# Order and tile shape of two small matmul groups ahead of a denominator, and the semaphore that a last multiply carries

## Chip, cores and metric

The kernel runs on one core of one Trainium2 chip. The metric is the device time of one execution in microseconds (us); a run also leaves a profile of one execution, whose span is about 1.6 us shorter than the device time (139.54 against 141.17 in the profiled run of the kernel before). Most executions agree within a few tenths of a microsecond (the kernel before: 141.01 to 141.78).

## The reference

```python
xn = layernorm(x)                                   # x: 2048 tokens x 448
q, k, v = split_heads(xn @ wqkv)                    # 16 heads of 28
phi = lambda t: where(t > 0, t + 1, exp(t)) + 1e-6
kv  = einsum("bhsd,bhse->bhde", phi(k), v)
z   = einsum("bhsd->bhd", phi(k))                   # sum of the keys over tokens
num = einsum("bhqd,bhde->bhqe", phi(q), kv)
den = einsum("bhqd,bhd->bhq", phi(q), z) + 1e-6
s   = merge_heads(num / den) @ wo
g   = silu(relu(xn @ w1 + b1)**2 @ w2 + b2)         # hidden size 1792
out = x + s * g
```

## The kernel before

The kernel records operations, and a small scheduler sets each engine's order and hands out the program's eight PSUM banks (`pb` in the traces): a bank keeps a sum of TensorE (PE) until another engine has read it, and only then goes to the next sum. PE takes its operations in the order in which they are added. Below are the parts that the change touches.

The hidden layer (h) and the second product (w_2, `gg`) run as phases: two sums side by side, one on rows 0 to 63 of the array, one on rows 64 to 127. Their tile shape is 64x128 (rows x columns).

```python
def token_sum(c):                   # xn^T phi(k), c = 3 is the last 64 rows
    for si in range(NT):            # NT = 16 token tiles
        if c < 3:
            ...                     # 128x128 tiles
        else:
            r = slice(64 * (si % 2), 64 * (si % 2) + 64)
            last = e.matmul(
                ps(b)[r, 0:D], xn[:, si, 384:448], pk_of(si), start=(si < 2), stop=(si >= NT - 2)
            )

def z_heads():                      # z per head, from zb, the keys summed over token tiles
    b = Buf("Z")
    def f(e, _):
        for r in range(4):
            for h in (0, 1):
                c, n = r * P + 64 * h, 1 + r // 3
                last = e.matmul(
                    ps(b)[half[h], r : r + n], zb[:, c : c + 64], ones[:, 0:n], start=(r == 0), stop=True,
                    skip_group_check=True,
                )
        return last
    add("pe", f, ["zb", "ones"], [b], 0.5)
    ...                             # VectorE: zsb = z * zmask
    add("dve", zops, [b, "zmask"], ["zsb"], 0.28)

def den():                          # denominators: 8 + 12 matmuls on 128x32 tiles, weights zsb
    ...

def finish(si, b, c):               # out tile = s (PSUM) * g
    ...
    if c.stop == D and c.start:     # the last multiply of the kernel
        op.lastly = "pe"            # this engine's wait stands last, on the instruction itself

# the order on PE
for i in range(3):
    phase((tail_h[i], K4), (tail_h[i + 3], K4))
g0, g1 = gg(0), gg(1)
for i in range(3):
    if i == 2:
        phase((g0, C), (g1, C))
    phase((tail_h[i + 3], K3), (tail_h[i], K3))
phase((g1, C), (g0, C))
z_heads()
token_sum(3)
den()
...
token_sum(0)                        # 128x128
```

An operation of this program with several waits gets separate wait instructions for all but one (EVENT_SEMAPHORE in the trace; 28 of them on VectorE in the profile before); the remaining wait is carried by the instruction itself. `lastly` picks that one.

## Time and profile before

| | before |
|---|---|
| median of 3 runs | 141.18 us (141.01 to 141.78) |
| profiled span | 139.54 us |
| first matmul of the 64x128 stream | 8.50 us |
| from there to the first 128x128 token sum | 69.05 us |
| from there to the last matmul's start | 59.36 us |
| from there to the end | 2.64 us |

The last four rows are my cut of the trace, by the starts of single matmuls; they add up to the span up to rounding. I call them head, middle, rest and tail. In a timeline a line gives start, length, engine, source line, operation, output and inputs, tile rows x columns, sizes and count. I call the time between the starts of like matmuls, pairs or waves in an unbroken row their stream: 0.216 us for 512 columns and 0.189 for 448 in the trace before. A matmul's recorded length is longer (about 0.38 and 0.35 us), so holes are found from starts: previous start plus stream against the next start. Tiles that run side by side form a pair (two, with starts 0.002 to 0.020 us apart in the trace before) or a wave (four, within 0.011). A number with three decimals is a start or an end in the trace's records, which a timeline prints with two.

### The profile page before, as it was taken

The page shows a single profiled execution, that of the slowest core. Times are in us where ns is not written, and L with a number is a line of the kernel's source. Part 1 is how long each engine was busy: PE and PEld are TensorE (multiplying, and loading weights), DVE is VectorE, ACT ScalarE, POOL GpSimd, SP SyncE. Part 2 cuts the span into 40 slices and gives each one's busy share as a digit, 9 for nine tenths or more (in the row PEclk, how much of TensorE's full clock was granted, in tenths as well). Part 3 has the DMA queues.
Part 4 walks back from the last instruction along what each step waited for, and adds up shares of the span by engine and source line. Part 5 has one row for each costly group of instructions (what it writes and reads, how often), then busy time and mean ns, then how long its engine had stood idle before and what let it go on. Part 6 is the DMA issues. An engine that isn't in the chain of part 4 may idle for free.

```text
span 139.5 us, 3096 instructions
## 1 busy us (share of the span) xinstructions
PE 136.6 (98%) x1255; PEld 72.4 (52%) x1255; DVE 92.3 (66%) x225; ACT 78.3 (56%) x153; POOL 26.8 (19%) x35
## 2 busy tenths in 40 slices
PE   9999999999999999999999999999999999999993
PEld 2484455555555555555555455645555555555472
DVE  3989797898888996889995900219836072452743
ACT  4779789788988878979788912512033030300221
POOL 2810000000000000000893000000001429092670
DMA  6997957999823300000000148970000102112132
GB/s 199 244 334 216 88 158 183 359 273 138 141 43 70 61 9 5 0 19 5 0 0 0 37 116 180 165 113 2 0 0 5 66 0 97 39 62 69 36 100 66
DMA packets 20353, 12.90 MB, mean 92 GB/s; under 512 B 9524, under 2 KB 19956, under 8 KB 20340
## 3 DMA queue, kind: packets, MB, share of 16 engines
q1 hardware_dynamic: 18332, 11.52, 35.8%
q10 hardware_dynamic: 2008, 1.19, 4.6%
q8 instruction: 10, 0.16, 0.5%
q14 instruction: 3, 0.02, 0.1%
HBM read 8.78 MB, written 2.10 MB: 78 GB/s over the span
## 4 chain that ended last, share of the span: by engine, by line
PE 95%; DVE 2%; DMA 2%; ACT 0%; issue 0%; DVEq 0%
PE pb L960 31%; PE pb L693 30%; PE pb L646 9%; PE pb L1028 8%; PE pb L727 7%; PE pb L677 6%; DMA x_tok<-in_A_x_dram 2%; PE pb L733 1%; PE pb L532 1%; DVE st L466 1%; PE pb L820 1%; PE pb L781 1%; PE pb L858 0%; DVE mv L467 0%; DVE xn L996 0%; PE pb L851 0%
## 5 line engine op out<-in xcount | busy, mean ns | idle before, releaser
L693 PE MATMUL pb<-xT,w 64*128 64x512 bf16 (+2 forms) x408 | 51.9, 365 | 0.0
L960 PE MATMUL pb<-w,r 64*128 64x448 bf16 (+3 forms) x406 | 44.9, 343 | 0.0
L702 ACT ACTIVATE r<-pb,b1f 128x512 bf16<-128x512 f32 x56 | 35.1, 688 | 3.7 <-PE pb L693 3.7
L693 PEld LDWEIGHTS pb<-xT,w 64*128 64x128 bf16 (+1 forms) x408 | 25.2, 94 | 19.3 <-issue 0.3
L960 PEld LDWEIGHTS pb<-w,r 64*128 64x128 bf16 (+1 forms) x406 | 23.1, 95 | 19.6 <-issue 0.7
L936 ACT ACTIVATE gbuf<-gbuf 128x448 bf16<-128x448 bf16 (+1 forms) x16 | 8.8, 567 | 36.3 <-DVE gbuf L971 35.7
L971 DVE TENSOR_TENSOR gbuf<-pb,b2b 128x448 bf16<-128x448 f32 (+1 forms) x16 | 9.3, 610 | 29.7 <-PE pb L960 29.7
L1007 POOL TENSOR_TENSOR xn<-xn,x_tok 128x448 bf16<-128x448 bf16 x15 | 15.1, 1032 | 46.3 <-DVE xn L996 46.3
L646 PE MATMUL pb<-w_qkv,xT 64*128 64x512 bf16 (+1 forms) x106 | 18.1, 377 | 0.0
L677 PE MATMUL pb<-xT,w_qkv 64*128 64x512 bf16 x84 | 15.6, 376 | 0.0
L710 DVE TENSOR_TENSOR r<-r 128x512 bf16<-128x512 bf16 x42 | 14.3, 419 | 0.0
L393 POOL MEMSET kvm<- 128x2048 bf16 x1 | 1.8, 1805 | 59.2 <-DVE zb L671 59.2
L1028 PE MATMUL pb<-msb,pqT 64*128 64x448 bf16 (+3 forms) x93 | 10.9, 343 | 0.0
L466 DVE BATCH_NORM_STATS2 st<-x_tok 128x6 f32<-128x448 bf16 x16 | 9.3, 612 | 2.4 <-DMA x_tok<-in_A_x_dram 2.3
L634 DVE SCALAR_TENSOR_TENSOR qk<-pb,qk 128x512 bf16<-128x512 f32 x16 | 10.6, 685 | 0.2
L624 ACT ACTIVATE qk<-pb 128x512 bf16<-128x512 f32 x16 | 8.9, 595 | 3.1 <-PE pb L646 2.5
L996 DVE TENSOR_TENSOR xn<-pb,gbuf 128x448 bf16<-128x448 f32 (+2 forms) x17 | 9.2, 591 | 1.8 <-ACT gbuf L936 1.3
L646 PEld LDWEIGHTS pb<-w_qkv,xT 64*128 64x128 bf16 (+1 forms) x106 | 7.1, 94 | 5.7 <-ACT xT L546 0.5
L727 PE MATMUL pb<-qk,xn 128*128 128x448 bf16 x48 | 9.3, 353 | 0.0
L677 PEld LDWEIGHTS pb<-xT,w_qkv 64*128 64x128 bf16 x84 | 6.3, 94 | 4.4
L711 ACT ACTIVATE r<-r 128x512 bf16<-128x512 bf16 x14 | 8.3, 635 | 0.0
L624 ACT ACTIVATE pqT<-pb 128x512 bf16<-128x512 f32 x12 | 6.8, 597 | 2.7 <-PE pb L693 1.6
(72 smaller groups left out, 101.9 us busy)
## 6 DMA issues: line engine op xcount, KB each, us to landing
out_dram<-xn SPq DMA_DIRECT2D x15, 112.0 KB, 1.7
w<-in_B_w_dram SPq DMA_DIRECT2D x1, 1568.0 KB, 10.3
x_tok<-in_A_x_dram SPq DMA_DIRECT2D x3, 448.0 KB, 3.8
xT<-rows ACTq DMA_DIRECT2D x6, 112.0 KB
w<-in_B_w_dram SPq DMA_DIRECT2D x1, 576.0 KB, 5.5
xT<-rows SPq DMA_DIRECT2D x5, 112.0 KB
w_o<-in_A_wo_dram SPq DMA_DIRECT2D x1, 392.0 KB, 11.4
w_qkv<-in_A_wqkv_dram SPq DMA_DIRECT2D x1, 384.0 KB, 3.5
```

Source lines behind the costliest of these rows:

```text
L466: add("dve", lambda e, _: e.bn_stats(st6[:, si, :], x_tok[:, si, :]), [("x", si)], [("st", si)], 0.58),
L624: add("act", lambda e, _: e.activation(out=slot, in_=src(), func=AF.Exp), [buf, "actw"], [tile], 0.6)
L634: lambda e, _: e.scalar_tensor_tensor(out=slot, in0=src(), scalar=1.0 + 1e-6, in1=slot, op0=ALU.add, op1=ALU.max),
L646: return e.matmul(ps(b)[:, 0:512], xT[half[h], c, si * P : (si + 1) * P], w_qkv[half[h], c, 384 : 2 * D], start=start, stop=stop,)
L677: return e.matmul(ps(b)[:, 0:512], w_qkv[half[h], c, m * P : (m + 1) * P], xT[half[h], c, g * 512 : (g + 1) * 512], start=start, stop=stop,)
L693: return e.matmul(ps(b)[:, c0 : c0 + n], w_1[half[h], c, fi * P : (fi + 1) * P], xT[half[h], c, t : t + n], start=start, stop=stop,)
L702: lambda e, _: e.activation(out=slot, in_=ps(b)[:, 0:512], func=AF.Relu, bias=b1f[:, fi : fi + 1]),
L710: return e.tensor_tensor(out=slot, in0=slot, in1=slot, op=ALU.mult)
L727: last = e.matmul(ps(b)[:, 0:D], xn[:, si, c * P : (c + 1) * P], pk_of(si), start=(si == 0), stop=(si == NT - 1),)
L960: return e.matmul(ps(b)[:, 0:n], r2[half[h], fi, si * P : (si + 1) * P], w_2[half[h], fi, c], start=start, stop=stop)
L1007: eng, lambda e, _: e.tensor_tensor(out=ob, in0=ob, in1=x_tok[:, si, c], op=ALU.add),
L1028: return e.matmul(ps(b)[:, 0:n], q, m, start=start, stop=stop)
```

## The change

The intent is to save changes of tile shape on PE: z takes the 64x128 shape of the phases and moves among them; the token sum of the last 64 rows takes the 128x32 shape of the denominators that follow it; and the last multiply no longer has a separate wait for ScalarE.

```diff
+        zlow = sb("zlow", [P, 5], f32)
@@ token_sum
-                        r = slice(64 * (si % 2), 64 * (si % 2) + 64)
-                        last = e.matmul(
-                            ps(b)[r, 0:D], xn[:, si, 384:448], pk_of(si), start=(si < 2), stop=(si >= NT - 2)
-                        )
+                        for i in (0, 1):
+                            r = 64 * (si % 2) + 32 * i
+                            last = e.matmul(
+                                ps(b)[r : r + 32, 0:D], xn[:, si, 384 + 32 * i : 416 + 32 * i], pk_of(si),
+                                start=(si < 2), stop=(si >= NT - 2), skip_group_check=True,
+                            )
@@ z_heads
-            b = Buf("Z")
+            bs = Buf("Z"), Buf("Z")
-                        c, n = r * P + 64 * h, 1 + r // 3
+                        n = 1 + r // 3
-                            ps(b)[half[h], r : r + n], zb[:, c : c + 64], ones[:, 0:n], start=(r == 0), stop=True,
+                            ps(bs[h])[:, r : r + n], zb[half[h], r * P : (r + 1) * P], ones[half[h], 0:n],
... VectorE: zlow = bs[0]; zlow = bs[1] + zlow; zsb = zlow * zmask
@@ finish
-                op.lastly = "pe"
+                op.lastly = "act"
@@ order on PE (behind the first three tail_h phases)
+        z_heads()
         g0, g1 = gg(0), gg(1)
@@ behind the last w_2 phase
         phase((g1, C), (g0, C))
-        z_heads()
         token_sum(3)
```

More of the change, by code (lines that the diff above doesn't have):

```diff
@@ L755, in f @@
                     for h in (0, 1):
-                        c, n = r * P + 64 * h, 1 + r // 3
+                        n = 1 + r // 3
                         last = e.matmul(
-                            ps(b)[half[h], r : r + n], zb[:, c : c + 64], ones[:, 0:n], start=(r == 0), stop=True,
-                            skip_group_check=True,
-                        )
-                return last
-            add("pe", f, ["zb", "ones"], [b], 0.5)
+                            ps(bs[h])[:, r : r + n], zb[half[h], r * P : (r + 1) * P], ones[half[h], 0:n],
+                            start=(r == 0), stop=True, skip_group_check=True,
+                        )
+                return last
+            add("pe", f, ["zb", "ones"], list(bs), 0.25)
+            add("dve", lambda e, _: e.tensor_copy(zlow[:, :], ps(bs[0])[:, 0:5]), [bs[0]], ["zlow"], 0.12)
+            add(
+                "dve",
+                lambda e, _: e.tensor_tensor(out=zlow[:, :], in0=ps(bs[1])[:, 0:5], in1=zlow[:, :], op=ALU.add),
+                [bs[1], "zlow"], ["zlow"], 0.12,
+            )
             def zops(e, _):
-                z = ps(b)[:, 0:5]
+                z = zlow[:, :]
                 z = bass.AP(tensor=z.tensor, offset=z.offset, ap=list(z.ap) + [[0, 32]])
                 return e.tensor_tensor(out=zsb[:, :, :], in0=z, in1=zmask[:, :, :], op=ALU.mult)
-            add("dve", zops, [b, "zmask"], ["zsb"], 0.28)
+            add("dve", zops, ["zlow", "zmask"], ["zsb"], 0.28)
         def fold_wv():
```

## The prediction

Passages of the text below are cut. One of them is a term of the sum: z's time in line, the author's estimate. The path after came to 2.69 us, the gain on PE to 0.14 and the whole sum to 0.20; the terms of the path that still stand (0.10 + 1.52 + 0.86 + 0.10) come to 2.58, and the cut term was the other 0.11. The spacing of 256-column waves is 0.109 us in the trace (76.682 to 76.791), not 0.107; that would add 0.004 to the path.

> **What bounds the kernel now.** I read the page first (busy times, slices, the chain that ended last), then the chain of waits in order of time for the two stretches that the diff touches, then the timeline of the TensorE in those stretches, in windows narrow enough to see single starts.
>
> ```profile
> span 139.5 us, 3096 instructions
> PE 136.6 (98%) x1255; PEld 72.4 (52%) x1255; DVE 92.3 (66%) x225; ACT 78.3 (56%) x153; POOL 26.8 (19%) x35
> PE 95%; DVE 2%; DMA 2%; ACT 0%; issue 0%; DVEq 0%
> ```
>
> TensorE (PE) is the bound: 98% busy and 95% of the chain. A stretch saved on another engine is worth nothing before the last matmul; a stretch saved on PE is worth itself, as long as nothing else catches up. The measured time, 141.18 us, is the span and about 1.7 us outside it. "Busy" hides small holes, because each record lasts longer than its stream (a 448-column matmul is recorded as 0.35 us, but 14 pairs of them take 2.65 us, 0.189 us a pair). So I looked for late starts: where a matmul or pair starts later than the previous start plus its stream. From 8.5 us to 136.9 us the trace has only a handful, each at a change of the tile's shape. Three stand in the stretch that the diff rewrites (timeline of PE; columns: start us, length us, engine, line, operation, tile rows*columns):
>
> ```profile
> 74.50 0.37 PE L960 MATMUL pb<-w,r 64*128 64x448 bf16 x2
> 74.80 0.29 PE L757 MATMUL pb<-ones,zb 128*64 128x1 bf16 x8
> 74.95 1.68 PE L733 MATMUL pb<-qk,xn 128*64 128x448 bf16 x16
> ...
> 76.28 0.35 PE L733 MATMUL pb<-qk,xn 128*64 128x448 bf16 x2
> 76.56 0.40 PE L851 MATMUL pb<-pqR,zsb 128*32 128x256 bf16 x8
> 76.79 0.82 PE L858 MATMUL pb<-pqT,zsb 128*32 128x512 bf16 x12
> 77.22 0.39 PE L858 MATMUL pb<-pqT,zsb 128*32 128x512 bf16 x4
> 77.54 0.36 PE L727 MATMUL pb<-qk,xn 128*128 128x448 bf16 x1
> ```
>
> The reader is to see: the last pair of 64x128 tiles starts at 74.50 and 74.52, so its stream is over at about 74.71, and the z sums (128x64) start at 74.80: 0.09 late. The last 128x64 pair starts at 76.28 and is over at 76.47; the 128x32 matmuls start at 76.56: 0.09 late. Their last wave starts at 77.22, takes 0.216 (the spacing of 512-column waves), is over at 77.44; the 128x128 matmul starts at 77.54: 0.10 late. The profile blames the second hole on a wait:
>
> ```profile
> 76.56 0.12 PEld L851 LDWEIGHTS pb<-pqR,zsb 128*32 128x32 bf16 x8 [0.36 <-DVE zsb L768]
> 75.98 0.32 DVE L768 TENSOR_TENSOR zsb<-pb,zmask 128x160 bf16<-128x160 f32 x1
> ```
>
> But zsb was done at 76.30, before the stream was, and the hole has the size of the others. I take it for a change of shape, not a wait. At the end of the kernel the chain of waits has these pieces (start us, us, what):
>
> ```profile
> 136.89 0.31 ACT gbuf L936
> 137.21 0.03 issue
> 137.24 0.02 DVEq L277
> 137.26 0.04 issue
> 137.30 0.34 DVE xn L996
> ```
>
> ScalarE's silu is over at 137.20; the multiply starts 0.10 later, after a separate wait instruction of VectorE (DVEq) and another issue gap. The multiply before it, whose own wait is on ScalarE, starts 0.04 after its silu (silu 135.86 + 0.44 = 136.30, multiply at 136.34).
>
> [...] The trace agrees, at about 0.09 to 0.10 us a change: the three above, and later 93.89 + 0.19 = 94.08 against 94.18. [...] The z sums stream one or two columns, and here their four pairs take 74.80 to 74.95, 0.15 us, 37 ns a pair[...]. [...] The trace shows it run ahead: the five wait instructions of the denominator's matmuls run at 74.9 to 75.3, while those matmuls start at 76.56. [...] The two multiplies above agree: 0.04 against 0.10.
>
> **The change, part by part.**
>
> z sums on halves. Removed: eight 128x64 matmuls at 74.80. Added: eight 64x128 matmuls (same count, one to two columns), between the first three and the next three h phases, near 67.47, into two banks, as two sums over 64 rows each; VectorE then copies one (5 columns), adds the other, and multiplies by the mask. On PE: 64x128 is the shape of the stream around them, so no change of shape comes in. [...] On VectorE: two small operations of about 0.18 us each (a 128x64 copy is 0.18 here), 0.36 us, inside a stretch where VectorE only squares r tiles and later sits idle 1.83 us before 74.91. Off the path.
>
> Last 64 rows of the token sum on 32-column tiles. Sixteen matmuls of 64 columns, two side by side, become 32 of 32 columns, four side by side. Before: 8 pairs at 0.189 = 1.51 us. After: 8 waves of four at 0.189 = 1.51 us, provided that four run together. The denominator's matmuls do that already: waves of four 512-column matmuls every 0.216 us. So the stream itself gains nothing, but it now has the shape of the denominator's matmuls behind it, and the change of shape between them goes: minus 0.09. The first wave after a change also comes about 0.01 late for its second (76.56 to 76.68 is 0.12 where 256 columns take 0.107); with one change fewer this goes too.
>
> The path before, from the end of the last 64x128 stream to the first 128x128 matmul: 74.71 to 77.54 = 2.83. After: [...] change of shape 0.10, token sum 1.52, denominators 2 x 0.107 + 3 x 0.216 = 0.86, change of shape 0.10: 2.69. Gain 0.14 us [...].
>
> Last multiply. Its wait on TensorE becomes the separate instruction, and ScalarE's is on the multiply itself. TensorE's last matmul (start 136.90) is done about 0.06 before the silu, so the separate wait is passed while the silu still runs. The gap of 0.10 becomes about 0.04: gain 0.06 us, wholly on the path since only the last residual add and the last store follow.
>
> Sum: 0.14 + 0.06 = 0.20 us, 0.14% of 141.18. Predicted 140.98 us.
>
> **The rivals.** Rival A, a new wait: the two z banks. The built order shows that the z sums take two banks that ScalarE must first empty, and that the first w_2 phase (68.77 before) takes those same two after VectorE has read them. ScalarE's four relus end at 64.43 + 2.42 = 66.85, zb is ready at 66.71 (and VectorE's new order has one zacc add of 0.66 less in front of it), z is due at 67.47: 0.6 us to spare. z is done by about 67.75; copy and add end by 68.2, or 68.5 if the four squares ahead are not moved earlier; the w_2 phase is due at 68.88: 0.4 to 0.7 to spare. If the first margin fails PE stalls some tenths and the gain is gone, 141.2 to 141.5.
> Rival B: the four 32-column tiles don't run together, since neighbours share the same keys or the loads double. Two at a time would be 16 x 0.189 = 3.0 us, 1.5 us lost, 142.5. The denominators speak against it.
> Rival C: the waits of the denominators are exposed, as twice the instructions now stand in the queue ahead of them. Five waits at about 0.1 are 0.5 us; [...].
> Rival D: the hole at 76.56 was a wait for zsb. Then too it goes, since zsb is ready some 6 us earlier; the number is the same, but the 128x64 to 128x32 change would not be its cause.
>
> **Range and chances.** The parts give 0.10 to 0.25 us of gain. The three runs of before spread from 141.01 to 141.78, more than the whole effect, so the range is run spread: 140.6 to 141.4. Faster by over 2% would need 2.8 us, which is nowhere in the diff; slower by over 2% needs rival B at nearly full serialisation. Chances: 0.005 faster, 0.985 within 2%, 0.01 slower.
>
> **What would show it.** In the changed kernel's timeline of PE: z pairs near 67.5 as 64x128 matmuls [...]; 32 token-sum matmuls over 1.51 us with one hole of 0.1 before them; the denominators' first matmul 0.19 after the last wave's start, without a hole; from the end of the w_2 phase to the first 128x128 token sum about 2.58 us; the last multiply about 0.04 after the silu, and no separate wait in the chain between. Wrong if PE shows a hole at z or at the first w_2 phase (A), waves wider than 0.189 (B), or a hole at the denominators (C); if the profile's span falls by less than 0.1 or by more than 0.3, a term of the sum is mis-sized.

## The result, and the profile after

The changed kernel took 141.07 us (median of 6 runs, 140.91 to 141.23) against 141.36 us for the kernel before (6 runs, 141.01 to 141.78, the three of the table above among them). The ratio is 0.9979 with a 95% interval from 0.9959 to 0.9999. Every ratio here is the mean time of one kernel's fast runs over the mean time of the fast runs of the kernel before, so it is not quite the ratio of the medians. A run is slow when it lies over 1.5% above the fastest of its kernel; none here did, and every profile told of has a granted TensorE clock of 1.0 in its record.

From the page of the changed kernel, busy times (the span is 139.4 us, and PE has 95% of the chain that ended last):

```profile
PE 136.4 (98%) x1271; PEld 69.3 (50%) x1271; DVE 92.9 (67%) x227; ACT 78.2 (56%) x153; POOL 22.9 (16%) x35
```

PE is still the bound, with 16 matmuls more and 0.2 us of busy time less. The next fence is the timeline of PE in narrow windows: first z in its new place, then the stretch that the prediction took apart.

```profile
67.31 0.38 PE L694 MATMUL pb<-xT,w 64*128 64x512 bf16 x2
67.52 0.25 PE L760 MATMUL pb<-ones,zb 64*128 64x1 bf16 x8
67.62 0.37 PE L694 MATMUL pb<-xT,w 64*128 64x512 bf16 x1
...
74.67 0.36 PE L969 MATMUL pb<-w,r 64*128 64x448 bf16 x2
74.96 1.70 PE L735 MATMUL pb<-qk,xn 128*32 128x448 bf16 x32
...
76.29 0.36 PE L735 MATMUL pb<-qk,xn 128*32 128x448 bf16 x4
76.48 0.39 PE L860 MATMUL pb<-pqR,zsb 128*32 128x256 bf16 x8
...
77.13 0.39 PE L867 MATMUL pb<-pqT,zsb 128*32 128x512 bf16 x4
77.45 0.36 PE L728 MATMUL pb<-qk,xn 128*128 128x448 bf16 x1
```

z starts exactly one stream after the pair before it (67.31 + 0.216) and the next h pair starts 0.104 us later: no hole at z, and 26 ns for each of its four pairs. The 32 matmuls of the token sum start at 74.96, which is 0.09 to 0.10 late (74.67 + 0.19 = 74.86), and take 1.52 us to the denominators' start, as eight waves of 0.189 should. The denominators start 0.19 after the last wave: the hole of 0.09 that stood here before is gone. The last hole, ahead of 77.45, is there as before.

The chain of waits at the end (start us, us, what):

```profile
136.80 0.31 ACT gbuf L945
137.12 0.04 issue
137.15 0.34 DVE xn L1005
```

The separate wait of VectorE no longer stands between the silu and the multiply: 0.04 us in place of 0.10. A separate wait is still there, but now it waits for TensorE. It ran from 137.086 to 137.107, and the silu ended at 137.108.

What now holds the multiply is most likely that wait. In all ten profiles, with either order, the multiply starts 44 to 45 ns after the end of its separate wait instruction. The two multiplies ahead of it carry ScalarE's wait themselves, with their other waits long done, and start 31 to 33 ns after the end of their silu in all ten. So about 0.01 us of the gap seems to be left to the wait for TensorE. No run here tests it.

In the cut by starts, before against after: head 8.50 and 8.57, middle 69.05 and 68.89, rest 59.36 and 59.36, tail 2.64 and 2.57. The middle gives 0.16 and the tail 0.06, together 0.22 us. Some 0.02 of the 0.16 is the uneven start of one pair: the two matmuls of the last w_2 pair start 0.020 apart in the profile before, and 0.003 to 0.009 apart in both profiles of the changed kernel and in e3 below. Up to the first 128x128 token sum e3 runs the same PE program as the kernel before, and its middle is 69.03. The head, which nothing in the diff touches, happened to be 0.07 longer in this profile, so the spans differ by only 0.15. In a second profile of the same changed kernel (e5 below) the head was 8.44, the middle 68.88 and the rest 59.36.

### The profile page after: what moved, and what is told of

It reads as the page before. It is cut to its first block, busy times and chain, and to the rows that moved or that the text cites. A ratio compares the mean times of both kernels' runs of the same rounds, so it can differ in the third digit from the quotient of the medians.

```text
span 139.4 us, 3131 instructions
## 1 busy us (share of the span) xinstructions
PE 136.4 (98%) x1271; PEld 69.3 (50%) x1271; DVE 92.9 (67%) x227; ACT 78.2 (56%) x153; POOL 22.9 (16%) x35
## 4 chain that ended last, share of the span: by engine, by line
PE 95%; DMA 2%; DVE 2%; ACT 0%; issue 0%
PE pb L969 31%; PE pb L694 30%; PE pb L647 9%; PE pb L1037 8%; PE pb L728 7%; PE pb L678 6%; DMA x_tok<-in_A_x_dram 2%; PE pb L735 1%; PE pb L533 1%; DVE st L467 1%; PE pb L829 1%; PE pb L790 1%; PE pb L867 0%; DVE mv L468 0%; DVE xn L1005 0%; ACT gbuf L945 0%
## 5 line engine op out<-in xcount | busy, mean ns | idle before, releaser
L694 PEld LDWEIGHTS pb<-xT,w 64*128 64x128 bf16 (+1 forms) x408 | 23.3, 94 | 21.0 <-DVE qk L635 0.3
L666 DVE TENSOR_TENSOR zacc<-zacc,qk 128x448 f32<-128x448 f32 x13 | 8.1, 623 | 0.3
```

Of the source, the lines that this page charges most:

```text
L694: return e.matmul(ps(b)[:, c0 : c0 + n], w_1[half[h], c, fi * P : (fi + 1) * P], xT[half[h], c, t : t + n], start=start, stop=stop,)
```

## The experiments

The theory: PE pays about 0.1 us for each change of tile shape, whatever is ready, and the change takes one away; z costs 26 ns a pair, as in the profile after; the separate wait costs 0.06. The main rival was that the hole ahead of the denominators had been a wait for zsb, as the profile says. Two batches of four kernels ran, each batch on one chip with its own runs of the kernel before (11 of them in each). All gave correct results.

| run | median us | ratio to before | 95% interval | middle us | silu end to multiply us |
|---|---|---|---|---|---|
| e1 z alone | 141.28 | 0.9991 | 0.9970 to 1.0013 | 69.00 | 0.10 |
| e2 token sum's tiles alone | 141.36 | 0.9999 | 0.9977 to 1.0022 | 69.22 | 0.10 |
| e3 last multiply alone | 141.18 | 0.9989 | 0.9968 to 1.0009 | 69.03 | 0.04 |
| e4 alternating shapes | 142.05 | 1.0039 | 1.0019 to 1.0060 | 69.71 | 0.04 |
| e5 changed kernel again | 140.94 | 0.9985 | 0.9971 to 0.9998 | 68.88 | 0.04 |
| e6 z moved, old form | 141.45 | 1.0011 | 0.9994 to 1.0027 | 69.11 | 0.04 |
| e7 z in halves, old place | 141.44 | 1.0017 | 1.0002 to 1.0032 | 69.31 | 0.04 |
| e8 z ten times | 142.03 | 1.0056 | 1.0037 to 1.0076 | 69.82 | 0.04 |

The kernel before had a median of 141.49 us in the batch of e1 to e4 and of 141.26 in that of e5 to e8. Effects below about 0.2% can't be read from the times, only from the traces.

### e1: z moved, the rest as before

```diff
 # the changed kernel, with
-    32-column tiles in token_sum(3)
+    the 64-column tiles of before
-                op.lastly = "act"
+                op.lastly = "pe"
```

> The changed kernel with the token sum back on 64-column tiles and the last multiply as before: z alone is moved. My theory (the hole ahead of the denominators is a change of tile shape): zsb is ready some 8 us early and the hole of 0.09 us ahead of the denominators' first matmul stays all the same; from the first matmul of the last w_2 pair to the first 128x128 matmul 2.88 us (before 3.04, changed kernel 2.78), z in line 0.10, so a gain over before of about 0.05 us, ratio 0.9996. Rival D (the hole was a wait for zsb): the hole is gone, the stretch is 2.78, gain 0.15 us, ratio 0.999.

Timeline of PE, and of its weight loads (PEld), at the denominators:

```profile
76.77 0.36 PE L734 MATMUL pb<-qk,xn 128*64 128x448 bf16 x2
77.05 0.40 PE L858 MATMUL pb<-pqR,zsb 128*32 128x256 bf16 x8
...
77.05 0.12 PEld L858 LDWEIGHTS pb<-pqR,zsb 128*32 128x32 bf16 x8 [0.36 <-issue]
```

zsb was done at 68.68 + 0.41 = 69.09, eight microseconds early, and the hole is still there: 76.77 + 0.19 = 76.96 against 77.05 (95 ns by single starts, 96 before). The same idle time that the profile had put down to zsb is now put down to "issue". The stretch from the last w_2 pair to the first 128x128 matmul is 2.90 us (2.88 expected). The 0.02 more is in the second pair of the token sum, which starts 0.213 behind the first in place of 0.189. So the hole was a change of shape, and the wait for zsb that the profile named was not its cause.

### e2: 32-column tiles alone

```diff
 # the kernel before, with the token_sum part of the diff only
```

> The kernel before with nothing but the 32-column token sum; z stays where it was, on 128x64 tiles. My theory: as many changes of shape as before (64x128, 128x64, 128x32, 128x128), only the middle one moves to stand ahead of the token sum, 0.09; no hole ahead of the denominators as long as zsb (ready at about 76.30) comes before they are due (about 76.56); stretch from the last w_2 pair to the first 128x128 matmul 3.02 to 3.05 us, gain 0.00, ratio 1.000. If the 32-column tiles themselves were faster, the stretch would fall below 2.9; if they don't run four together it would be 4.5.

```profile
74.72 0.37 PE L962 MATMUL pb<-w,r 64*128 64x448 bf16 x2
75.02 0.29 PE L759 MATMUL pb<-ones,zb 128*64 128x1 bf16 x8
75.23 1.70 PE L734 MATMUL pb<-qk,xn 128*32 128x448 bf16 x32
76.76 0.39 PE L853 MATMUL pb<-pqR,zsb 128*32 128x256 bf16 x8
```

The token sum takes 1.53 us to the denominators, without a hole between them, but z and the token sum now have different shapes: from z's first matmul to the token sum's first it is 0.22 us, where it was 0.15 before. The stretch is 3.02 us, against 3.04. One hole has moved; none has gone. By one measure for all, from the end of the last w_2 pair's stream to the first 128x128 matmul, with z's time added where z was moved, it is 2.83 us before (2.83 in e3), 2.81 in e1, 2.81 in e2 and 2.69 in the changed kernel (2.69 in e5). So z moved saves 0.02 alone, the narrow tiles 0.03 alone, and both together 0.14. The counts of changes of shape fit: three on this path before, in e1 and in e2, and two in the changed kernel. (The middle of this run is longer than that of before, because PE waited 0.20 us for ScalarE at 16.7 us, long ahead of the changed part. That wait is in one profile only.)

### e3: the last multiply alone

```diff
 # the kernel before, with
-                op.lastly = "pe"
+                op.lastly = "act"
```

> The kernel before with nothing but ScalarE's semaphore on the last multiply itself. My theory: from the end of the last silu to the multiply's start 0.04 us instead of 0.10, no separate wait in the chain, gain 0.06 us, ratio 0.9996, too small for the timed rounds to show. Rival (the multiply is held by TensorE's last matmul, or by something else): the gap stays 0.10.

```profile
137.27 0.31 ACT gbuf L936
137.58 0.04 issue
137.62 0.34 DVE xn L996
```

The separate wait is gone from the chain and the gap is 0.04 us, as expected. Here too the wait for TensorE ended, at 137.571, only just before the silu, at 137.572. The tail, from the last matmul's start to the end, is 2.58 us against 2.64 with the old order. The timed ratio of 0.9989 does not contradict it, but can't show it either.

### e4: seven changes of shape more

```diff
 # the changed kernel, token_sum(3)
-                        for i in (0, 1):
-                            r = 64 * (si % 2) + 32 * i
+                        n = 64 if (si // 2) % 2 == 0 else 32
+                        for i in range(64 // n):
+                            r = 64 * (si % 2) + n * i
     ... tiles of n columns in place of 32
```

> The changed kernel with the token sum's eight pairs of tiles alternately on 64-column and 32-column tiles: the same sums, seven changes of shape more. My theory (about 0.10 us a change: 0.09 of hole and 0.01 in the second wave): the stretch from the last w_2 pair to the first 128x128 matmul is 2.78 + 0.7 = 3.5 us, the time 0.7 us longer than the changed kernel's, ratio to before about 1.003. Rival (a hole comes from waits, not from shapes): no holes between the pairs, 2.8 us, ratio 0.998.

```profile
75.01 0.38 PE L736 MATMUL pb<-qk,xn 128*64 128x448 bf16 x2
75.32 0.68 PE L736 MATMUL pb<-qk,xn 128*32 128x448 bf16 x6
75.62 0.68 PE L736 MATMUL pb<-qk,xn 128*64 128x448 bf16 x5
```

(Each line starts at one of the alternating groups; its count runs on into the next.) The groups start about 0.31 us apart instead of 0.189. The stretch is 3.60 us against 2.78, so seven changes cost 0.82, or 0.117 us each: more than the 0.10 that I took. The time agrees: 0.39% over before, where the changed kernel is 0.15% to 0.21% under it, some 0.54% to 0.60% or 0.8 us. This is the one run in which the cost of a change of shape is clear of the noise of the times.

### e5: the changed kernel again

The edit is none; it is the yardstick of e6 to e8.

> The changed kernel once more, on the chip of the next three, so that they are compared with it in the same rounds: 0.15 to 0.3 us less than before, ratio 0.998 to 0.999; the stretch from the last w_2 pair to the first 128x128 matmul 2.78 us again, z in line 0.10, silu to multiply 0.04.

The stretch is 2.78 us, z takes 0.103, the gap ahead of the multiply 0.04, and the ratio is 0.9985. The two batches of the changed kernel agree.

### e6: z in the new place, in the old form

```diff
 # the changed kernel, with z_heads() as before (128x64 tiles, one bank), called in the new place
```

> The changed kernel with z in its new place but in the old form (128x64 tiles, one bank, no addition). My theory: two changes of shape come into the 64x128 stream, so z takes 0.09 + 0.15 + 0.10 = 0.34 us of it instead of 0.10; the time 0.24 us longer than the changed kernel's, about that of before. Rival (the form of z does not matter, only its place): 0.10 to 0.15 us, the time of the changed kernel.

```profile
67.78 0.38 PE L694 MATMUL pb<-xT,w 64*128 64x512 bf16 x2
68.08 0.29 PE L760 MATMUL pb<-ones,zb 128*64 128x1 bf16 x8
68.31 0.39 PE L694 MATMUL pb<-xT,w 64*128 64x512 bf16 x2
```

From the end of the stream before z (67.78 + 0.22 = 68.00) to the next h pair it is 0.31 us (0.34 expected), where the halves take 0.10. The middle is 0.22 us longer than in e5 (69.11 against 68.88, from unrounded values), so z on halves is what keeps the shape of the stream. The scheduler also moved one eviction (a copy out of PSUM) from ScalarE to VectorE in this kernel and one squaring of r the other way; PE shows no hole from it. The ratio to e5 is 1.0011 / 0.9985 = 1.0026, or 0.37 us, which is of the right sign and larger than the trace has it; the two intervals overlap. This profile's head was also long, 9.04 us.

### e7: z on halves, in the old place

```diff
-        z_heads()
         g0, g1 = gg(0), gg(1)
...
         phase((g1, C), (g0, C))
+        z_heads()
         token_sum(3)
```

> The changed kernel with z on its two 64-row halves but in the old place, behind the last w_2 phase. My theory: no change of shape more than in the changed kernel, but zsb now comes from three operations of VectorE behind two evictions of gbuf, ready at about 76.85 where the denominators are due at about 76.4: a true wait of 0.4 us ahead of them, no longer the 0.09 of a change; stretch from the last w_2 pair to the first 128x128 matmul 3.3 us, time 0.4 us longer than the changed kernel's and 0.2 longer than before. Rival (place does not matter): stretch 2.89 (z in it), time of the changed kernel.

Timelines of PE and VectorE (DVE):

```profile
75.06 1.70 PE L735 MATMUL pb<-qk,xn 128*32 128x448 bf16 x32
76.92 0.29 PE L860 MATMUL pb<-pqR,zsb 128*32 128x256 bf16 x4 [0.17 <-DVE zsb L777]
...
75.08 1.16 DVE L980 TENSOR_TENSOR gbuf<-pb,b2b 128x448 bf16<-128x448 f32 x2 [1.84 <-PE pb L969]
76.16 0.15 DVE L767 COPY zlow<-pb 128x5 f32<-128x5 f32 x1
76.34 0.16 DVE L770 TENSOR_TENSOR zlow<-pb,zlow 128x5 f32<-128x5 f32 x1
76.54 0.33 DVE L777 TENSOR_TENSOR zsb<-zlow,zmask 128x160 bf16<-128x160 f32 x1
```

This is what a true wait for zsb looks like. The three operations stand behind two evictions, zsb is done at 76.87, and the denominators start at 76.92, although the token sum's stream was over 0.34 us earlier with the same tile shape on both sides. PE itself, not only the weight loads, is shown idle with zsb as the releaser. The stretch is 3.23 us (3.3 expected). So the two parts of the z edit need each other: on halves z costs two operations more on VectorE (0.15 and 0.16 us here), and only the early place hides them.

### e8: z ten times

```diff
-                for r in range(4):
+                for r in 10 * list(range(4)):
```

> The changed kernel with the eight z matmuls issued ten times over (each time from the start flag, so the result is the same). My theory (about 26 ns a pair, on the path): z takes 1.04 us of the stream, the time 0.94 us longer than the changed kernel's, ratio to it 1.0067. Rival (z hides behind the 512-column stream or in the queue): the time of the changed kernel.

```profile
67.37 1.16 PE L760 MATMUL pb<-ones,zb 64*128 64x1 bf16 x80
68.37 0.37 PE L694 MATMUL pb<-xT,w 64*128 64x512 bf16 x1
```

Eighty matmuls, that is 40 pairs, take 1.00 us of the stream: 25 ns a pair. The ratio to e5 is 1.0056 / 0.9985 = 1.0071, or 1.0 us. The middle is 0.94 us longer than in e5 (69.82 against 68.88), for 36 pairs more: z's cost is wholly on the path and is not hidden behind the streams around it.

## Why the prediction was right

Point by point, by its own steps:

- TensorE as the bound: the rest of the trace behind the changed part, from the first 128x128 token sum to the last matmul, is 59.36 us in the kernel before, in the changed one and in all eight experiments. Whatever was saved or lost ahead of it went through unchanged.
- z in line (the cut term, 0.11 of the 2.69): 0.15 us before, 0.104 in the first profile after, 0.103 in the second, and e8 shows 25 ns a pair when it is repeated.
- Token sum's stream unchanged and one change of shape fewer: 1.52 us and no hole at the denominators. From the end of the w_2 phase (74.86) to the first 128x128 matmul it is 2.59 us in both profiles; 2.58 was forecast.
- The gain on PE of 0.14, the cut term in it: 0.14 by the prediction's own path (2.83 to 2.69), in both profiles of each order; 0.16 by the middle, of which 0.02 is the uneven pair. The hole that went was 0.09 to 0.10, as read, but e4 measures 0.117 per added change.
- The last multiply for 0.06: 0.06, and e3 shows it alone. One reading behind it was off, and here there was luck: the wait for TensorE was to be passed 0.06 ahead of the silu's end, but that counted from the modelled end of the last matmul (137.043 in the changed kernel). The wait instruction starts 0.043 after that end and takes 0.021, so the margin was 0.001. A little later, and the gain would have shrunk.
- Sum 0.20 us: 0.20 by the prediction's own path, 0.22 by the cut; 0.3 and 0.2 us by the two timed ratios, with intervals that reach almost to zero. The forecast of 140.98 us against 141.07 measured says little by itself, since the kernel before moved by as much between its batches.
- Rival A (a new wait at the two z banks): it did not occur. z was issued without a hole, and the addition that frees the second bank was done at 68.18, where the w_2 phase started at 68.92.
- Rival B (32-column tiles not four together): refuted by the eight waves of 0.189.
- Rival C (the denominators' waits exposed): refuted. The five wait instructions ran at 75.2 to 75.6, 0.8 us ahead of the matmuls that they guard.
- Rival D (the hole was a wait): refuted by e1. The profile puts the two other holes before down to waits as well, of weight loads for ScalarE (`r` ahead of 74.80, `at` ahead of 77.54), but what it names was done at 74.56 and 77.22, ahead of the ends of the streams at 74.71 and 77.44.

What stays open is what the 0.1 us is spent on: the three holes before end with the weight loads of the new shape and its first matmul starting together (within 0.01 us), and no run here separates the two. The 0.117 of e4 is less of a riddle than it looks. With the late second wave or pair counted in, a single change costs 0.109 into 128x32 (0.097 + 0.012, before) and 0.118 into 128x64 (0.094 + 0.024, e1).

No experiment points to a kernel that beats the changed one: each part taken out or altered lengthens the middle or the tail.

## What to carry to other kernels

On a TensorE-bound kernel, list the changes of tile shape on its path: each cost about a tenth of a microsecond here (0.09 to 0.12 us), which the busy share did not show (98% before and after) and which the profile put down to a wait at all three holes before. A small matmul group can perhaps take the shape of its neighbours, as two did here, for 0.14 of 141 us. A group that takes its neighbour's shape at the price of more work on another engine may have to move earlier too, or a true wait takes the place of the hole (0.34 us in e7). To tell the two apart, make the input ready far too early and see whether the hole stays. And the wait that was moved off the last multiply did not vanish: it ended 0.001 us ahead of the silu (137.107 and 137.108). Look at how close two such waits come.

## What the traces show beside the result

- Changes of tile shape: a hole of 0.09 to 0.11 us at each single change behind a full-length stream among 64x128, 128x64, 128x32 and 128x128 (in the trace before 0.090, 0.097 and 0.105 at 74.80, 76.56 and 77.54), 0.07 to 0.09 behind the z sums (e2, e6, e7), 0.01 to 0.02 us more in the wave behind it (before, e1), and 0.117 us for each of seven in a row (e4).
- Short matmuls: with two row tiles side by side (64x128), 80 one- and two-column matmuls took 1.00 us, 25 ns a pair (e8). On 128x64 tiles the z pairs took 37 ns in the mean of four (53 for the first, 32 for the others, in the trace before).
- Waits of VectorE: with a separate wait for ScalarE ahead of the last multiply it was 0.10 us from the end of the silu to the start of the multiply (before), against 0.03 (31 to 33 ns, at two multiplies of each of the ten profiles) where the multiply carries that wait itself, and 0.044 to 0.045 us from the end of a separate wait instruction to the start of the multiply behind it.
- The releaser that the profile names at a change of tile shape can be a false one: the hole ahead of the denominators was put down to zsb (before), and to "issue" once zsb was eight microseconds early (e1), at the same 0.36 us of idle time.

Unexpected: of the four parts of the trace, the head is the one that varies on its own. Over the ten profiles it ran from 8.40 to 9.04 us, while the rest, 59 us long, repeated to within 0.01 us. (The middle had an early wait of its own in two profiles: 0.20 us at 16.7 us in e2, 0.08 us at 11.5 us in e7.) In the profile with one of the longest heads (e1) the chain went back to a weight load (`w`, 5.07 us from 1.45) in place of the first load of x.

So two versions of this kernel compare far more sharply by the parts of their traces than by their times.
